# Four batches of sorted block attention and a token mixer on one core: another order of loads and work, V of one batch turned on TensorE, X of two batches turned by DMA

## The chip, the core and the metric

The kernel runs on one core of a Trainium2 chip. A core has five engines with queues of their own, each working strictly in order: PE (TensorE, matrix products), DVE (VectorE), ACT (ScalarE), POOL (GpSimd) and SP (SyncE, which here only issues transfers). [...] Loads that change the type are issued by POOL; all transfers run on 16 DMA engines. The metric is the device time of one execution in microseconds (us).

## The reference

There are B = 4 batches, H = 8 heads, S = 768 rows and D = 64. A row of 768 is cut into 8 blocks of 96.

```python
P = sort_net                                  # [4, 8, 8, 8]
for _ in range(5):
    P = P - max(P, -1); P = exp(P)
    P = P / (sum(P, -1) + 1e-09)
    P = P / (sum(P, -2) + 1e-09)
k_sorted = einsum('bhij,bhjcd->bhicd', P, k_blocks)      # the same for v
scores = (q_block @ k_sorted_block.T) / sqrt(D)          # 96 x 96 in each block
attn = softmax(scores)
x = (attn @ v_sorted_block)  -> [B, S, H*D]              # [4, 768, 512]

wq, wk = x @ w_q, x @ w_k                                # 64 columns each
mixed = (wq @ wk.T / sqrt(64)) @ x                       # 768 x 768, no softmax
out = relu(mixed) @ w_out                                # float32 [4, 768, 512]
```

The kernel computes `wq @ (wk.T @ x)`, with the 64 x 512 matrix in brackets first.

## The kernel before

The whole order of work is written out by hand in the string `ORDER`, and a loop at the end of the function calls one small function `u_<letter>` for each word. A word such as `K03:6` is a PE step: letter K, batch 0, index 3, first PSUM bank 6. A word such as `k03:A:6` is the step that empties that bank, on ACT (`A`) or DVE (`D`); `G` is POOL and `S` is SP. Since each engine works in order, `ORDER` is at once the queue of each engine: a step that waits holds all later steps of its own engine, and the others run on until they need it.

The steps of a batch, in the order in which data flows:

- `lq`, `lk`, `lv`: the load of Q, K or V of a batch (1.5 MB of float32 in memory, 768 KB as bf16) on POOL's queue into one of three buffers; `lp` loads w_q and w_k, `lo` w_out.
- `a`, `c`: the five rounds of normalizing P (exponential on ACT, the rest on DVE); `B` and `n` spread the result into the mask products M (128 x 128 for each head) which sort the blocks by a matrix product. `n00` to `n03` (batch 0) are on DVE, those of later batches on POOL.
- `Q`, `q`: Q turned on PE (12 products a step, for two heads) and copied to QT. `K`, `k`: K sorted and turned in one product with M, copied to KT. `S`, `e`: scores of five head-pair blocks, exponential on ACT into E.
- `V`, `v`: V sorted by M into Vs; `R`: six transfers a batch on SP's queue that regroup Vs into VT (rows of a block on the partitions). VT has a column of ones for the sums of the softmax. `N`: a copy of one column of VT on POOL, a gate that waits for the six transfers.
- `P`: E times VT, 14 products a step (8 in `P_4`); `r`, `x`: reciprocal of the sums and the scaled result into X on DVE.
- `T`, `t`: X turned on PE (8 products for a pair of heads) and copied to XT. `J`, `j`: wq and wk together into qkT; `d` copies the wq half to the other 64 partitions (qD). `W`, `w`, `G`, `g`: the 64 x 512 matrix. `H`, `h`: mixed and relu. `O`, `o`: product with w_out (4 products of 512 columns) and its copy to an output tile; `s`: the store.
- `i`: constants. `i00` makes the identity on POOL, `i02` some zeros on DVE, and `i03` on POOL the pads of E, the columns of ones in Vs and VT and a corner of Rall. `Z019` is 19 products of zeros that fill PE's queue.

Buffers of batch b are used again by batch b + 2, those of the loads (`Qn`, `Kn`, `Vn`) by batch b + 3. `u_Y`, `u_y`, `u_F`, `u_f` (L276 to L289) are in the file before the change, but no word of `ORDER` calls them. After the last step a guard on POOL (L438 to L449) checks the range of Rall and would run a slow general path; it does not here.

Of the kernel before, what the change touches and what calls it, by code (L numbers as in the profile page):

```python
# [9 lines left out]
BF16 = mybir.dt.bfloat16  # L10
# [4 lines left out]
NMIX = 2  # L15

ORDER = """
i02:D c00:D i00:G lq0 a01:A c01:D a02:A c02:D Z019:0 Q03:0 a03:A c03:D a04:A Q00:1 c04:D Q02:2 lq1
a05:A c05:D lv0 Z010:3 B00:3 lk0 n00:D:3 q00:A:1 n03:D:3 n02:D:3 Q13:1 i03:G Q11:4 q02:A:2 q03:D:0
Q12:2 q13:A:1 n01:D:3 Q01:5 Z011:6 V01:6 V00:0 q12:D:2 v00:A:0 u00:D:3 q01:D:5 V02:2 Q10:5 lk1  # L20
v02:A:2 Z09:0 K00:0 K01:2 n10:G q10:D:5 q11:A:4 K02:4 v01:A:6 K03:6 k00:A:0 lv1 k01:D:2 n11:G
k03:A:6 S00:0 k02:D:4 S01:2 S06:6 S04:4 e01:A:2 Z03:2 K10:2 e00:A:0 K13:0 e06:A:6 R01:S S02:6
k10:D:2 k13:D:0 K12:2 S05:0 e04:A:4 n21:G S03:4 R00:S R04:S e02:A:6 k12:D:2 lk2 e05:A:0 R03:S K11:6
lq2 e03:A:4 R02:S R05:S n20:G S14:2 e14:A:2 V12:0 k11:D:6 v12:D:0 V10:6 P03:4 r03:D:4 x03:D:4 V11:2
S11:0 v10:A:6 v11:A:2 P01:6 e11:A:0 P02:4 S12:2 S13:0 r01:D:6 x01:D:6 e12:A:2 r02:D:4 K22:6 k22:A:6
K20:2 e13:A:0 P04:6 x02:D:4 S15:4 e15:A:4 k20:D:2 P00:2 S10:0 r04:D:6 Q23:4 x04:D:6 R14:S r00:D:2
Q20:5 S16:6 e10:A:0 N05:G R15:S R10:S Q22:0 x00:D:2 Q21:3 q20:D:5 e16:A:6 K23:1 K21:5 T01:7 R11:S
q22:D:0 lv2 R12:S R13:S q23:A:4 k21:A:5 q21:D:3 lp k23:D:1 P12:3 t01:A:7 T02:0 r12:D:3 P11:5
x12:D:3 r11:D:5 V20:1 lq3 T03:7 t02:A:0 T00:0 V21:3 v20:A:1 x11:D:5 P13:1 t00:D:0 t03:A:7 P14:5
v21:A:3 r13:D:1 T11:7 J01:0 V22:3 x13:D:1 r14:D:5 j01:A:0 x14:D:5 P10:1 v22:A:3 r10:D:1 t11:D:7  # L30
n30:G x10:D:1 J00:0 S23:5 S20:3 T12:7 lk3 j00:A:0 e23:A:5 t12:D:7 e20:A:3 T13:0 W01:1 W00:2 n31:G
T10:5 S24:6 w01:D:1 t13:D:0 w00:D:2 S22:3 S25:0 t10:D:5 R23:S Q30:2 e24:A:6 Q31:5 Q33:6 N15:G G00:7
e22:A:3 q30:D:2 e25:A:0 Q32:2 d01:S K32:3 lv3 q31:D:5 q33:D:6 K31:5 K33:0 G01:7 q32:D:2 R20:S
k32:A:3 R24:S k31:A:5 k33:D:0 d00:S S21:2 J10:4 e21:A:2 g00:D:7 R25:S R21:S j10:D:4 S35:5 H02:0 lo
e35:A:5 R22:S H00:2 h00:A:2 J11:7 K30:4 j11:A:7 h02:D:0 k30:D:4 S32:0 W10:6 V30:2 w10:D:6 W11:7
V32:4 e32:A:0 P23:0 w11:A:7 v32:A:4 V31:6 v30:D:2 r23:D:0 v31:A:6 O04:2 x23:D:0 R31:S P20:3 S26:0
r20:D:3 R34:S S30:5 G10:7 G11:7 e26:A:0 S33:0 x20:D:3 H01:3 e30:A:5 o04:A:2 g10:D:7 P21:5 O05:2
h01:A:3 P22:3 d11:S r21:D:5 x21:D:5 T20:7 o05:A:2 e33:A:0 r22:D:3 t20:A:7 P24:5 R35:S x22:D:3
r24:D:5 O03:2 d10:S o03:A:2 O00:0 S36:3 H10:1 R32:S x24:D:5 S31:5 o00:A:0 R30:S e31:A:5 O02:7
h10:D:1 T22:0 e36:A:3 o02:A:7 t22:D:0 S34:5 s02:S H11:1 H12:3 R33:S T21:7 e34:A:5 N25:G O01:0  # L40
t21:A:7 P33:5 h11:D:1 T23:7 P30:1 h12:A:3 t23:A:7 o01:D:0 r33:D:5 P32:3 x33:D:5 s00:S r30:D:1 J20:0
O12:5 r32:D:3 s01:S P31:6 x30:D:1 j20:D:0 x32:D:3 O10:1 r31:D:6 O11:0 J21:4 j21:A:4 P34:2 x31:D:6
T32:6 o10:A:1 d21:S T31:7 r34:D:2 t31:A:7 T30:4 W20:1 N35:G x34:D:2 t30:A:4 T33:2 t32:D:6 t33:D:2
O15:3 J30:4 w20:D:1 W21:1 J31:2 j30:A:4 W30:4 j31:D:2 O14:7 W31:2 o11:A:0 w21:A:1 G20:1 o14:A:7
d30:D w30:A:4 s10:S d20:S G21:1 w31:D:2 G30:4 o15:A:3 G31:4 g20:A:1 o12:A:5 H20:6 h20:A:6 H22:2
H21:0 d31:D g30:D:4 h22:D:2 O13:4 O21:7 o13:A:4 s11:S h21:D:0 O20:6 o20:A:6 H30:2 s12:S H31:4
h31:A:4 o21:D:7 O24:7 O25:6 O22:4 h30:D:2 O23:5 O31:3 o25:A:6 o23:A:5 o24:D:7 s20:S o22:D:4 H32:0
O30:4 s22:S o31:D:3 O33:3 s21:S h32:D:0 o33:D:3 o30:A:4 O35:0 O34:1 o34:A:1 s31:S O32:3 s30:S
o35:D:0 o32:A:3 s33:S s35:S s34:S s32:S
"""  # L50


# [1 line left out]
def kernel(  # L54
# [91 lines left out]
    def mm(o, w, x, start=True, stop=True, t=False):  # L146
        nc.tensor.matmul(o, w, x, is_transpose=t, start=start, stop=stop, skip_group_check=True)  # L147

    def copy(e, o, i):
        if e == "A":  # L150
            nc.scalar.copy(o, i)  # L151
        else:
            nc.vector.tensor_copy(o, i)  # L153
# [7 lines left out]

    def u_a(b, n, e, bank):
        nc.scalar.activation(Pv, Pv, ACT.Exp)
        if n == 2:
            for j in range(NB):
                mm(PS[:, 7, 0:SP], idb, idb[:, j * SP:(j + 1) * SP], start=(j == 0), stop=(j == NB - 1))
            nc.scalar.copy(m_p, PS[:, 7, 0:SP])
        elif n == 3:
            nc.scalar.copy(Lx.rearrange("p a j s -> p (a j) s"),
                           idb[0:BH, 0:BH].unsqueeze(2).to_broadcast([BH, BH, SP]))  # L170

    def u_c(b, n, e, bank):
        if n == 0:
# [46 lines left out]
                                in_=src[b, h0:h1].rearrange("h (p r) d -> p h (r d)", p=P))  # L220

    def u_B(b, n, bank):

        for i in range(NB):
            g, x = divmod(i, BH // NB)
            mm(PS[:, bank, i * BH:(i + 1) * BH], Lx[:, x].rearrange("p j s -> p (j s)"),
               PbT[:, g * BH:(g + 1) * BH])
# [74 lines left out]
        ENG[e].dma_start(out=VT[b % 2].rearrange("(s r) i h x -> r s i (h x)", r=R6)[n],  # L302
                         in_=Vs[0][:, n].rearrange("p h e -> p (h e)"))

    def u_N(b, n, e, bank):

        nc.gpsimd.tensor_copy(gate[0:R6, :], VT[b % 2][0:R6, NB - 1, H - 1, 0:1])  # L307
# [111 lines left out]
    def oslot(b, n):  # L419
        return ot[(b * 3 + n // 2) % NOT]  # L420
# [4 lines left out]
    def u_s(b, n, e, bank):  # L425
# [220 lines left out]
```

## Time and profile before

| | |
|---|---|
| median of 3 runs | 111.21 us (110.87 to 113.28) |
| span of the profiled execution, first to last instruction | 109.3 us |
| mean granted PE clock over that span | 0.966 |
| first Q of batch 0 usable on PE | 8.97 us |
| K of batch 0 usable on PE | 21.1 us |
| first V step of batch 3 on PE | 62.88 us |
| last product on PE starts its group of 20 | 100.84 us |

The profile is that of one execution. Times are from its first instruction. Engines' busy times overlap. A row of the timeline reads: start, length, engine, line, operation, output and input, count, and in brackets how long the engine stood idle and what ended it. A row of a group reads: operation, shapes, count, then total busy time, mean length of one in ns, then idle time ahead of the group. Nearly every PE row has the line L147 and every copy L151 (ACT) or L153 (DVE), since these are helpers; the tiles' names tell the steps apart. The digits of the slices are tenths, 40 slices of 2.73 us.

The loads of before are issued by POOL in the order q0, q1, v0, k0, k1, v1, k2, q2, v2, w_q, w_k, q3, k3, v3, w_out, with `i03`, the products `n` and the gates between them.

### The profile page before, as it was taken

The numbers are of one execution on the slowest core, as the hardware profiler recorded it, in microseconds if no ns is written. First come the engines' busy times: TensorE is split into PE (matmuls) and PEld (weight loads), VectorE is DVE, ScalarE is ACT, GpSimd is POOL, SyncE is SP. The second block draws the span as 40 slices with busy tenths as digits, with TensorE's granted clock in tenths as the row PEclk, the third lists the DMA queues.
The fourth block names the chain that finished last, engine by engine and source line by source line (L and its number), as shares of the span: only waits on it lengthen the run. The fifth ranks groups of instructions, "written<-read, shape, count | busy, mean of one in ns | idle before, by whom it ended". The sixth has DMA issues, their size and how long they took to land.

```text
span 109.3 us, 3462 instructions
## 1 busy us (share of the span) xinstructions
PE 94.8 (87%) x1460; PEld 64.3 (59%) x1460; DVE 71.1 (65%) x140; ACT 67.6 (62%) x96; POOL 26.8 (24%) x46
## 2 busy tenths in 40 slices
PE   4997999986978759999959999999999993999950
PEld 2335557463767648897948687746858672443410
DVE  2676681060959984799956898778898431974720
ACT  4224314897589874698976998899706671463240
POOL 7960029069079700330000000000004700000000
PEclk9999999999599995999999999999999999999999
DMA  0899999999999999999999914670360050097872
GB/s 3 91 201 204 203 204 206 203 235 248 229 210 199 218 254 239 188 209 202 218 242 248 201 25 117 164 244 6 127 261 17 6 218 4 40 418 309 352 307 112
DMA packets 20225, 20.16 MB, mean 185 GB/s; under 512 B 2032, under 2 KB 18288, under 8 KB 20208
## 3 DMA queue, kind: packets, MB, share of 16 engines
q0 software_dynamic: 14064, 10.09, 61.1%
q1 hardware_dynamic: 6144, 9.84, 26.7%
q8 instruction: 11, 0.18, 0.6%
q14 instruction: 6, 0.05, 0.1%
HBM read 20.19 MB, written 6.29 MB: 242 GB/s over the span
## 4 chain that ended last, share of the span: by engine, by line
PE 53%; DMA 34%; POOL 5%; issue 2%; DVE 2%; ACT 1%; POOLq 0%; ACTq 0%; DVEq 0%
PE ps L147 53%; DMA Kn<-in_k_dram 15%; DMA Qn<-in_q_dram 14%; DMA qD<-qkT 4%; POOL Qn L219 2%; POOL M L240 1%; DVE QT L153 1%; DVE KT L153 1%; POOL Kn L219 1%; POOL Vn L219 1%; ACT ot L151 1%; POOL idb L191 0%; POOL idb L190 0%; POOLq L191 0%; DVE qkT L153 0%
## 5 line engine op out<-in xcount | busy, mean ns | idle before, releaser
L321 ACT ACTIVATE E<-ps 96x960 bf16<-96x960 f32 (+1 forms) x28 | 24.1, 898 | 5.2 <-PE ps L147 5.1
L147 PE MATMUL ps<-wo,mixT 128*128 128x512 bf16 x96 | 22.7, 379 | 0.0
L350 DVE TENSOR_TENSOR X<-ps,Rall 96x896 bf16<-96x896 f32 (+1 forms) x20 | 20.1, 1005 | 0.6
L151 ACT COPY ot<-ps 128x512 f32<-128x512 f32 x17 | 10.0, 588 | 8.7 <-PE ps L147 8.0
L147 PE MATMUL ps<-fil 128*128 128x512 bf16 x52 | 14.4, 433 | 0.4 <-ACT Vs L151 0.2
L153 DVE CAST KT<-ps 128x768 bf16<-128x768 f32 x10 | 9.4, 956 | 7.7 <-PE ps L147 7.5
L147 PEld LDWEIGHTS <-mixT 128*128 128x128 bf16 x96 | 8.6, 98 | 9.4 <-issue 0.6
L151 ACT CAST Vs<-ps 128x1024 bf16<-128x1024 f32 x10 | 9.9, 1019 | 4.2 <-PE ps L147 4.0
L147 PE MATMUL ps<-VT,E 96*128 96x65 bf16 x256 | 10.9, 193 | 1.0 <-DVE X L350 0.3
L147 PEld LDWEIGHTS <-E 96*128 96x128 bf16 x256 | 9.8, 97 | 2.8 <-issue 1.3
L147 PE MATMUL ps<-idb,Qn 128*64 128x128 bf16 x192 | 8.1, 244 | 3.3 <-DMA Qn<-in_q_dram 1.9
L240 POOL TENSOR_TENSOR M<-PTR,m_p 128x512 bf16<-128x512 bf16 x6 | 7.9, 1323 | 12.1 <-DVE PTR L153 8.4
L412 DVE TENSOR_SCALAR mixT<-ps 128x1024 bf16<-128x1024 f32 x7 | 8.5, 1222 | 3.0 <-PE ps L147 3.0
L147 PE MATMUL ps<-QT,KT 64*128 64x96 bf16 x256 | 10.0, 213 | 0.4 <-DVE KT L153 0.2
L153 DVE COPY QT<-ps 128x768 bf16<-128x768 bf16 x11 | 5.9, 553 | 6.7 <-PE ps L147 6.7
L307 POOL COPY gate<-VT 6x1 bf16<-6x1 bf16 x4 | 0.7, 177 | 38.3 <-DMA VT<-Vs 38.3
L147 PEld LDWEIGHTS <-fil 128*128 128x128 bf16 x52 | 5.4, 109 | 7.4 <-issue 3.4
L147 PEld LDWEIGHTS <-Qn 128*64 128x64 bf16 x192 | 6.7, 124 | 4.6 <-DMA Qn<-in_q_dram 2.7
L147 PE MATMUL ps<-M,Kn 128*64 128x128 bf16 x192 | 8.0, 238 | 1.6 <-DMA Kn<-in_k_dram 1.3
L147 PEld LDWEIGHTS <-KT 64*128 64x128 bf16 x256 | 6.9, 99 | 3.5 <-issue 1.9
L147 PEld LDWEIGHTS <-Kn 128*64 128x64 bf16 x192 | 6.7, 121 | 3.5 <-DMA Kn<-in_k_dram 2.2
L147 PE MATMUL ps<-idb,X 96*128 96x96 bf16 x128 | 7.5, 206 | 0.0
(74 smaller groups left out, 129.0 us busy)
## 6 DMA issues: line engine op xcount, KB each, us to landing
out_dram<-ot SPq DMA_DIRECT2D x9, 512.0 KB, 3.3
VT<-Vs SPq DMA_DIRECT2D x24, 132.0 KB, 6.4
Qn<-in_q_dram POOLq DMA_DIRECT2D x4, 768.0 KB, 12.8
Vn<-in_v_dram POOLq DMA_DIRECT2D x4, 768.0 KB, 14.9
Kn<-in_k_dram POOLq DMA_DIRECT2D x4, 768.0 KB, 18.1
out_dram<-ot SPq DMA_DIRECT2D x6, 256.0 KB, 2.0
wo<-in_moe_w_out_dram POOLq DMA_DIRECT2D x1, 512.0 KB, 17.4
qD<-qkT SPq DMA_DIRECT2D x6, 48.0 KB, 3.3
```

Source lines behind the costliest of these rows:

```text
L147: nc.tensor.matmul(o, w, x, is_transpose=t, start=start, stop=stop, skip_group_check=True)
L151: nc.scalar.copy(o, i)
L153: nc.vector.tensor_copy(o, i)
L219: nc.gpsimd.dma_start(out=t[b % NIN][:, h0:h1].rearrange("p h r d -> p h (r d)"), in_=src[b, h0:h1].rearrange("h (p r) d -> p h (r d)", p=P))
L240: ENG[e].tensor_tensor(out=M[b % 2][:, h0:h0 + hn], in0=src.unsqueeze(2).to_broadcast([P, hn, SP, NB]), in1=m_p.unsqueeze(1).unsqueeze(3). ...
L307: nc.gpsimd.tensor_copy(gate[0:R6, :], VT[b % 2][0:R6, NB - 1, H - 1, 0:1])
L321: nc.scalar.activation(E[b % 2][:, n, 0:2 * w * BLK].rearrange("p (t a c) -> p a t c", a=2, c=BLK), PS[0:BLK, bank:bank + 2, 0:w * BLK].re ...
L350: nc.vector.tensor_mul(xo.rearrange("p (a t d) -> p a t d", a=2, d=D), avps(bank, w)[:, :, :, 0:D], Rall[:, b, n, :, 0:w].unsqueeze(3).to_ ...
L412: nc.vector.tensor_relu(o, i)
```

## The change

1. POOL's queue: all of q0, k0, v0, q1, k1, v1, w_q, w_k, q2, k2, v2, w_out, q3 are issued first, then `i03`, then the products `n` of batch 1 and 2 with k3 and v3 between.
2. The gates `N` are gone; `P` waits for the transfers itself.
3. V of batch 0 takes the steps `Y`, `y`, `F`, `f`: sorted and turned by 48 products with M, copied to the KT buffer of the other batch, turned back by 32 products and copied to VT. The six transfers `R` of batch 0 and its `V`, `v` are gone.
4. X of batches 2 and 3 is turned by `D`, a transposing transfer from SP's queue for each pair of heads, in place of `T` and `t` (eight steps each).
5. `d` of batches 0 to 3 is a copy on DVE or POOL throughout; before, six of the eight were transfers on SP's queue.
6. The product and copy for `m_p` and the copy for `Lx` are words of `ORDER` (`B01`, `p00`, `p01`). The products of zeros go from 52 to 24.
7. The whole of `ORDER` is new, with other banks and another split of copies between ACT and DVE.

```diff
-i02:D c00:D i00:G lq0 a01:A c01:D a02:A c02:D Z019:0 Q03:0 a03:A c03:D a04:A Q00:1 c04:D Q02:2 lq1
-a05:A c05:D lv0 Z010:3 B00:3 lk0 n00:D:3 q00:A:1 n03:D:3 n02:D:3 Q13:1 i03:G Q11:4 q02:A:2 q03:D:0
...
+i00:G i02:D B01:0 lq0 Z08:1 c00:D lk0 p01:A a01:A p00:A:0 lv0 c01:D lq1 a02:A c02:D lk1 Z010:0 lv1 a03:A c03:D
+lp a04:A lq2 Q01:0 c04:D Q02:1 q01:A:0 Q03:2 lk2 Q00:3 q03:D:2 Z03:4 a05:A q00:A:3 lv2 c05:D Z03:0 lo q02:D:1
+lq3 B00:0 n03:D:0 i03:G n01:D:0 K03:1 n00:D:0 K01:3 n02:D:0 k03:A:1 u00:D:0 K00:5 k01:D:3 n11:G S05:0 k00:A:5
+S02:2 e05:A:0 n10:G S06:4 Y03:6 e02:A:2 S01:0 y03:D:6 e01:A:0 S00:2 Y01:6 e06:A:4 Y00:0 y01:D:6 e00:A:2 F03:4
+n20:G f03:A:4 F01:7 Q12:2 f01:D:7 y00:A:0 Q11:3 P04:4 q11:A:3 Q13:7 r04:D:4 Q10:6 x04:D:4 q12:A:2 F00:0
+q10:D:6 q13:A:7 Y02:3 f00:D:0 K02:5 y02:D:3 k02:A:5 lk3 P00:0 r00:D:0 S04:6 lv3 x00:D:0 P01:4 e04:A:6 S03:2
...
+D23:S e34:A:2 S35:0 G11:6 D22:S e35:A:0 S32:4 s02:S g10:D:6 S36:2 O03:7 e32:A:4 H11:0 o03:D:7 e36:A:2 P33:4
+h11:A:0 s01:S P31:6 r33:D:4 P32:2 x33:D:4 O12:0 r32:D:2 r31:D:6 H10:4 x32:D:2 o12:A:0 O13:1 h10:A:4 x31:D:6
+D32:S J20:0 P34:2 j20:D:0 J21:4 D31:S r34:D:2 d20:D P30:5 x34:D:2 j21:A:4 W20:0 O10:7 r30:D:5 d21:G D33:S
+w20:D:0 x30:D:5 W21:0 o10:A:7 G20:2 w21:D:0 D30:S o13:D:1 H12:3 G21:2 h12:D:3 s11:S O11:1 g20:A:2 H20:6
+o11:A:1 H21:4 h20:D:6 O15:3 h21:A:4 s10:S O14:2 o15:A:3 O21:7 o14:A:2 J31:6 s12:S o21:A:7 J30:5 j31:A:6 O22:7
...
-    gate = sb.tile([P, 1], BF16, name="gate")
...
         nc.scalar.activation(Pv, Pv, ACT.Exp)
-        if n == 2:
-            for j in range(NB):
-                mm(PS[:, 7, 0:SP], idb, idb[:, j * SP:(j + 1) * SP], start=(j == 0), stop=(j == NB - 1))
-            nc.scalar.copy(m_p, PS[:, 7, 0:SP])
-        elif n == 3:
-            nc.scalar.copy(Lx.rearrange("p a j s -> p (a j) s"),
-                           idb[0:BH, 0:BH].unsqueeze(2).to_broadcast([BH, BH, SP]))
+
+    def u_p(b, n, e, bank):
+        if n == 0:
+            copy(e, m_p, PS[:, bank, 0:SP])
+        else:
+            copy(e, Lx.rearrange("p a j s -> p (a j) s"),
+                 idb[0:BH, 0:BH].unsqueeze(2).to_broadcast([BH, BH, SP]))
...
     def u_B(b, n, bank):
-
+        if n == 1:
+            for j in range(NB):
+                mm(PS[:, bank, 0:SP], idb, idb[:, j * SP:(j + 1) * SP], start=(j == 0), stop=(j == NB - 1))
+            return
...
-    def u_N(b, n, e, bank):
-
-        nc.gpsimd.tensor_copy(gate[0:R6, :], VT[b % 2][0:R6, NB - 1, H - 1, 0:1])
-
...
+    def u_D(b, n, e, bank):
+        ENG[e].dma_start_transpose(out=XT[b % 2][:, n, :].rearrange("p (i c) -> p i c", i=NB),
+                                   in_=X[b % 2][:, n].rearrange("p i m -> p (i m)"))
+
...
-        if e == "S":
-            nc.sync.dma_start(out=o, in_=i)
+        if e == "G":
+            nc.gpsimd.tensor_copy(o, i)
```

More of the change, by code (lines that the diff above doesn't have):

```diff
@@ L17 @@
 ORDER = """
-i02:D c00:D i00:G lq0 a01:A c01:D a02:A c02:D Z019:0 Q03:0 a03:A c03:D a04:A Q00:1 c04:D Q02:2 lq1
-a05:A c05:D lv0 Z010:3 B00:3 lk0 n00:D:3 q00:A:1 n03:D:3 n02:D:3 Q13:1 i03:G Q11:4 q02:A:2 q03:D:0
[L20 to L47, printed above, removed]
@@ L48 @@
-O30:4 s22:S o31:D:3 O33:3 s21:S h32:D:0 o33:D:3 o30:A:4 O35:0 O34:1 o34:A:1 s31:S O32:3 s30:S
-o35:D:0 o32:A:3 s33:S s35:S s34:S s32:S
+i00:G i02:D B01:0 lq0 Z08:1 c00:D lk0 p01:A a01:A p00:A:0 lv0 c01:D lq1 a02:A c02:D lk1 Z010:0 lv1 a03:A c03:D
+lp a04:A lq2 Q01:0 c04:D Q02:1 q01:A:0 Q03:2 lk2 Q00:3 q03:D:2 Z03:4 a05:A q00:A:3 lv2 c05:D Z03:0 lo q02:D:1
+lq3 B00:0 n03:D:0 i03:G n01:D:0 K03:1 n00:D:0 K01:3 n02:D:0 k03:A:1 u00:D:0 K00:5 k01:D:3 n11:G S05:0 k00:A:5
+S02:2 e05:A:0 n10:G S06:4 Y03:6 e02:A:2 S01:0 y03:D:6 e01:A:0 S00:2 Y01:6 e06:A:4 Y00:0 y01:D:6 e00:A:2 F03:4
@@ new lines @@
+n20:G f03:A:4 F01:7 Q12:2 f01:D:7 y00:A:0 Q11:3 P04:4 q11:A:3 Q13:7 r04:D:4 Q10:6 x04:D:4 q12:A:2 F00:0
+q10:D:6 q13:A:7 Y02:3 f00:D:0 K02:5 y02:D:3 k02:A:5 lk3 P00:0 r00:D:0 S04:6 lv3 x00:D:0 P01:4 e04:A:6 S03:2
+n21:G r01:D:4 e03:A:2 K10:0 x01:D:4 F02:7 k10:A:0 f02:D:7 K12:2 S10:0 k12:A:2 P03:6 V12:4 e10:A:0 r03:D:6
+V10:2 x03:D:6 v10:A:2 P02:0 v12:D:4 T03:7 T00:6 R10:S t03:A:7 V11:2 r02:D:0 t00:D:6 R14:S K13:4 v11:A:2
+x02:D:0 R15:S K11:6 n31:G k13:A:4 R11:S k11:D:6 T02:0 R12:S n30:G S16:1 S14:3 t02:A:0 R13:S S12:5 T01:7
@@ new lines @@
+e12:A:5 Q20:0 t01:D:7 q20:A:0 J00:7 e14:A:3 S13:5 j00:D:7 J01:0 e13:A:5 d00:D S15:3 j01:D:0 W00:7 e15:A:3
+Q21:6 d01:G w00:D:7 W01:0 q21:D:6 e16:A:1 Q23:7 w01:A:0 K23:3 q23:A:7 K22:1 K20:5 k22:D:1 k23:A:3 G00:7
+k20:D:5 Q22:0 S26:1 q22:A:0 P13:3 S20:5 e26:A:1 r13:D:3 G01:7 x13:D:3 e20:A:5 S24:0 g00:A:7 S25:5 e24:A:0
+P12:3 e25:A:5 r12:D:3 V20:0 x12:D:3 v20:A:0 V22:6 P14:4 v22:A:6 H00:2 R20:S r14:D:4 K21:0 x14:D:4 R21:S
+h00:A:2 V21:6 R24:S H01:4 v21:D:6 k21:A:0 R25:S O01:3 h01:A:4 S22:0 R22:S o01:D:3 S23:6 e22:A:0 T13:2 R23:S
@@ new lines @@
+S21:4 T12:3 e23:A:6 S11:0 t12:D:3 e11:A:0 Q32:6 Q31:3 q32:D:6 Q30:7 t13:A:2 q31:D:3 P10:0 q30:A:7 Q33:6
+r10:D:0 P11:2 x10:D:0 q33:A:6 O00:7 e21:A:4 r11:D:2 x11:D:2 H02:0 O02:6 o00:A:7 h02:D:0 s00:S T10:7 o02:A:6
+T11:2 P24:3 t10:A:7 t11:D:2 P22:5 r24:D:3 P21:0 x24:D:3 J11:7 r22:D:5 r21:D:0 x22:D:5 K31:2 j11:A:7 O05:4
+k31:A:2 d11:D x21:D:0 W11:5 K33:6 w11:A:5 K30:2 o05:D:4 k33:A:6 D21:S P20:0 J10:5 k30:A:2 r20:D:0 x20:D:0
+V32:6 j10:A:5 V30:2 v32:A:6 d10:D V31:4 D20:S v30:D:2 K32:0 v31:A:4 R35:S S31:6 k32:D:0 R34:S S30:2 e31:A:6
@@ new lines @@
+P23:4 R33:S S33:0 e30:A:2 r23:D:4 R32:S W10:6 x23:D:4 O04:7 R30:S e33:A:0 w10:D:6 R31:S S34:2 o04:A:7 G10:6
+D23:S e34:A:2 S35:0 G11:6 D22:S e35:A:0 S32:4 s02:S g10:D:6 S36:2 O03:7 e32:A:4 H11:0 o03:D:7 e36:A:2 P33:4
+h11:A:0 s01:S P31:6 r33:D:4 P32:2 x33:D:4 O12:0 r32:D:2 r31:D:6 H10:4 x32:D:2 o12:A:0 O13:1 h10:A:4 x31:D:6
+D32:S J20:0 P34:2 j20:D:0 J21:4 D31:S r34:D:2 d20:D P30:5 x34:D:2 j21:A:4 W20:0 O10:7 r30:D:5 d21:G D33:S
+w20:D:0 x30:D:5 W21:0 o10:A:7 G20:2 w21:D:0 D30:S o13:D:1 H12:3 G21:2 h12:D:3 s11:S O11:1 g20:A:2 H20:6
@@ L50 @@
+o11:A:1 H21:4 h20:D:6 O15:3 h21:A:4 s10:S O14:2 o15:A:3 O21:7 o14:A:2 J31:6 s12:S o21:A:7 J30:5 j31:A:6 O22:7
+d31:D j30:A:5 d30:D W31:6 W30:5 o22:D:7 O20:4 w31:A:6 w30:D:5 G30:5 o20:D:4 H22:6 G31:5 s20:S h22:A:6 O23:4
+g30:A:5 O24:7 o23:D:4 H30:5 s21:S o24:D:7 H31:3 h30:A:5 O25:2 h31:D:3 H32:0 o25:A:2 O30:7 h32:D:0 s22:S O32:6
+o30:A:7 O34:0 s30:S o32:A:6 O33:7 s32:S o34:D:0 O31:6 s34:S o33:D:7 O35:0 s33:S o31:A:6 s31:S o35:A:0 s35:S
 """
@@ L609 @@
         b, n = int(name[1]), int(name[2:])
-        if kind.isupper() and kind not in "RN":
+        if kind.isupper() and kind not in "RD":
             fns[kind](b, n, int(arg[0]))
```

## The prediction

> **What bounds the kernel now.** I read the page's busy line and slices first, then the chain of waits in order of time, then busy time by stretch.
>
> ```profile
> PE 94.8 (87%) x1460; PEld 64.3 (59%) x1460; DVE 71.1 (65%) x140; ACT 67.6 (62%) x96; POOL 26.8 (24%) x46
> PEclk9999999999599995999999999999999999999999
> DMA  0899999999999999999999914670360050097872
> ```
>
> PE is busiest, but its share is an average. The DMA digit is 9 from the third slice to the 23rd, so up to about 60 us the loads stream without a gap; from there PE is full. The clock digit falls to 5 twice, at 27 and 41 us, both times beside a wait for a load (below).
>
> ```profile
> 4.36 16.73 DMA Kn<-in_k_dram
> 24.93 15.54 DMA Qn<-in_q_dram
> 63.68 23.30 PE ps L147 x353
> 87.55 4.50 DMA qD<-qkT
> 92.09 13.25 PE ps L147 x75
> ```
>
> The chain waits for K of batch 0 until 21.09 us, then for Q of batch 2 until 40.47, then runs on PE with one break for the qD transfer. Three stretches of before, cut at K10 (26.4), V30 (62.88) and P33 (76.60), and the end behind the last matmul:
>
> ```profile
> 26.40:62.88 36.48, 31.96 (x707) 26.78 (x707) 28.19 (x46) 28.09 (x35) 9.81 (x13) 0.91 1.29 220
> 62.88:76.60 13.72, 13.70 (x224) 9.48 (x222) 11.33 (x17) 12.51 (x19) 0.18 (x1) 1.00 0.38 110
> 76.60:105.33 28.73, 26.99 (x265) 15.66 (x263) 18.55 (x30) 13.11 (x23) 3.23 (x7) 1.00 0.45 180
> 105.33:109.30 3.97, 0.00 (x0) 0.00 (x0) 0.00 (x0) 0.59 (x1) 0.00 (x0) 0.93 0.51 194
> ```
>
> Columns: length, then PE, PEld, DVE, ACT, POOL busy, clock, DMA, GB/s. In the second stretch PE is never idle and ACT is busy 12.51 of 13.72 us, 91%: two engines are nearly full there, and ACT has little to give.
>
> **The change, stage by stage.** I split the new kernel at P04 (the first P on PE) and at P33.
>
> *Start to P04.* Rows for the loads and POOL's queue:
>
> ```profile
> 1.48 2.03 POOL L219 DMA_DIRECT2D Qn<-in_q_dram  x2 [0.17 <-issue]
> 8.97 1.03 PEld L147 LDWEIGHTS <-Qn 128*64 128x64 bf16 x36 [1.27 <-DMA Qn<-in_q_dram]
> 12.82 1.37 PEld L147 LDWEIGHTS <-Qn 128*64 128x64 bf16 x48 [0.19 <-DMA Qn<-in_q_dram]
> 5.22 0.32 POOL L200 MEMSET E<- 96x224 bf16 x1
> 6.27 0.90 POOL L219 DMA_DIRECT2D Kn<-in_k_dram  x1
> 12.77 1.09 DVE L240 TENSOR_TENSOR M<-ps,m_p 128x256 bf16<-128x256 f32 x3 [0.85 <-PE ps L147]
> ```
>
> q0 is usable at 8.97 and q1, next in the queue, at 12.82: 3.85 us a load; up to k0, the fourth, it is (21.09 - 8.97)/3 = 4.04. With q0, k0, v0 ahead, k0 lands at about 12.9 instead of 21.1, just as the mask products M (12.77) are ready. So the long first wait goes, and E of batch 0 is done some 7 us sooner. What is late next is on POOL. The memsets i03, issued at 5.22 before, now stand behind lq3. In the built program the loads share eight completion counters in turn, so lq3, the thirteenth, waits for the fifth, k1: 8.97 + 4 x 3.85 to 4.04 = 24.4 to 25.1. Its issue takes 0.90 and the memsets 6.27 - 5.22 = 1.05, so they end at 26.4 to 27.1; I take 26.5. P04 reads the columns of ones in VT and waits for them. All else on PE stands behind P04: Q13, Q10, F00, Y02, K02, and so S04 and the next E. V of batch 0 by Y and F (48 + 32 matmuls for 24) and the 28 fillers taken out lie in this idle time and cost nothing; the six R transfers of batch 0 go as well. If P04 did not wait, Y and F would still be hidden, because q1 lands only at 8.97 + 3 x 3.85 = 20.5.
>
> M of batch 1 stands behind lq3 too, and the gates are gone:
>
> ```profile
> 15.60 1.31 POOL L240 TENSOR_TENSOR M<-PTR,m_p 128x512 bf16<-128x512 bf16 x1 [8.43 <-DVE PTR L153]
> L307 POOL COPY gate<-VT 6x1 bf16<-6x1 bf16 x4 | 0.7, 177 | 38.3 <-DMA VT<-Vs 38.3
> VT<-Vs SPq DMA_DIRECT2D x24, 132.0 KB, 6.4
> ```
>
> n11 and n10 end at 26.5 + 2 x 1.31 = 29.1; K10, the first to use them, stands behind S03 and can't start before 30.7, so they are hidden. The gates made POOL wait 38.3 us off the path and held lv2 and later loads behind the R transfers; now P waits for the six transfers itself and the loads run beside them. R of batch 1 is issued from about 37 and takes 6.4 us and some more, P13 comes near 47: hidden.
>
> The price of the fillers is the clock: the two low slices follow idle times of 1.05 and 1.13 us in these rows, and here PE stands for about 5 us.
>
> ```profile
> 26.42 1.14 PE L147 MATMUL ps<-M,Kn 128*64 128x128 bf16 x24 [1.05 <-DMA Kn<-in_k_dram]
> 40.51 1.49 PE L147 MATMUL ps<-idb,Qn 128*64 128x128 bf16 x24 [1.13 <-DMA Qn<-in_q_dram]
> 57.69 1.19 PE L147 MATMUL ps<-M,Kn 128*64 128x128 bf16 x36
> ```
>
> 24 matmuls take 1.14 us in the low slice, 36 take 1.19 at full clock. From P04 to S04 PE has 88 (8+12+12+8+12+12+14+10): 2.9 us at the one pace, 4.2 at the other. I take the slow one: ACT gets its next E at 26.5 + 4.2 = 30.7. [...]
>
> *P04 to P33.* At 26.5 the two kernels have PE work of about the same size behind them (fillers apart), but not the same ACT work ahead. From 26.5 to P33 the new order gives ACT 20 long and 3 short E, 9 KT, 6 QT, 6 Vs, 4 XT, 3 ot, 2 mixT, 2 qkT and three small copies.
>
> ```profile
> L321 ACT ACTIVATE E<-ps 96x960 bf16<-96x960 f32 x24 | 22.6, 967 | 2.8 <-PE ps L147 2.7
> L321 ACT ACTIVATE E<-ps 96x384 bf16<-96x384 f32 x4 | 1.9, 484 | 2.4 <-PE ps L147 2.4
> L151 ACT CAST KT<-ps 128x768 bf16<-128x768 f32 x6 | 4.7, 800 | 3.2 <-PE ps L147 3.2
> L151 ACT COPY QT<-ps 128x768 bf16<-128x768 bf16 x5 | 3.9, 791 | 1.8 <-PE ps L147 1.8
> L151 ACT CAST Vs<-ps 128x1024 bf16<-128x1024 f32 x10 | 9.9, 1019 | 4.2 <-PE ps L147 4.0
> L151 ACT COPY XT<-ps 128x768 bf16<-128x768 bf16 x8 | 6.3, 806 | 0.1
> L151 ACT COPY ot<-ps 128x512 f32<-128x512 f32 x17 | 10.0, 588 | 8.7 <-PE ps L147 8.0 <-ACT wk L151 0.8
> L410 ACT ACTIVATE mixT<-ps 128x1024 bf16<-128x1024 f32 x5 | 5.1, 1028 | 2.3 <-PE ps L147 2.3
> L151 ACT CAST qkT<-ps 128x384 bf16<-128x384 f32 x5 | 2.4, 478 | 5.7 <-PE ps L147 5.6
> ```
>
> At busy time over count: 18.8 + 1.4 + 7.1 + 4.7 + 5.9 + 3.2 + 1.8 + 2.0 + 1.0, and 1.1 for the small ones (three, bounded by 0.5 each) = 47.0 us, against 28.09 + 12.51 = 40.6 in before's stretch from K10 to P33. PE's share there was 31.96 + 13.70 = 45.7 with nearly the same items, so ACT is the fuller of two full engines, and DVE has less. E36 (0.5) is not needed for P33 and q13 and k02 (1.6) run before 30.7; 44.9 us are left. At 91%, the rate of before's fullest stretch, they take 49.4; with no gaps 44.9; I take 94%, 47.8, since ACT is now the engine in front rather than the one behind. P33 then starts at 30.7 + 47.8 = 78.5 (75.6 to 80.1), against 76.60 before. The loads do not bound it: the same bytes, less six R transfers, end near 60 as before, and Q20, K23, V20 and Q32 come after their loads by several us at ACT's pace.
>
> *P33 to the end.* Of PE's items behind P33 the new order lacks five T and has two H more; all else is the same, 18 O among it.
>
> ```profile
> L147 PE MATMUL ps<-idb,X 96*128 96x96 bf16 x128 | 7.5, 206 | 0.0
> L147 PE MATMUL ps<-qkT,Ab 64*128 64x256 bf16 x24 | 3.9, 271 | 0.0
> 92.09 0.28 PE L147 MATMUL ps<-qD,Ab 64*128 64x256 bf16 x1 [1.74 <-DMA qD<-qkT]
> ```
>
> T: 40 x 7.5/128 = -2.3; H: 4 pairs x 3.9/24 = +0.65; the qD wait of 1.74 goes, since d20 and d21 are now copies on DVE and POOL. 28.73 - 2.3 + 0.65 - 1.74 = 25.3 us, then the same 3.97. What could come late instead are the transposing transfers: J20 needs D22 and D23, J31 needs all four of batch 3. D30 waits for x30. P30's place puts that some 7.5 us behind P33 (three pairs r, x on DVE, then r34, x34, then r30, x30), at 86.2, and J31 stands about 11.7 us of PE work behind P33, at 90.2.
>
> ```profile
> out_dram<-ot SPq DMA_DIRECT2D x6, 256.0 KB, 2.0
> qD<-qkT SPq DMA_DIRECT2D x6, 48.0 KB, 3.3
> ```
>
> No trace shows a transposing transfer. By bytes, 192 KB, the nearest rows are 2.0 us for 256 KB and 3.3 for the 48 KB between partitions; by pieces it writes 128 x 8 lines, as many as a load has packets, at 3.85 us apiece. I take 3.3 from issue to landing, and that four in a row follow each other faster than that: D30 lands at 89.5, just hidden. D22 and D23 are issued early, behind R31, and have more room. [...]
>
> Sum: 78.5 + 25.3 + 4.0 = 107.8 us of span, 1.5 below 109.3. The median of the runs, 111.21, lies 1.9 above the profiled span; so 109.7.
>
> **Rivals.** *ACT does not bind, or POOL does not hold P04.* With no gaps on ACT P33 comes at 75.6, the span is 104.9, the time 106.8. If lq3 were issued without waiting, P04 would follow Q11 at about 21.5; M for batch 1, two products on POOL, would then be early too, and the end could move by up to 5 us, to 104.7. For it: ACT does 91% where it isn't even first. Against: banks are reused at once, so a late copy on either engine stops PE, and the wait on the fifth counter stands in the program.
>
> *The transposes are slow, and the kernel is slower.* At 3.85 us each, one behind the other on SP's queue, with D32 issued when x31 is done (about 83), four take to 98.4 and J31 starts 8 us late: time 118. It decides from about 1.75 us apiece. [...] Against: SP's queue holds little else then, and the loads are over.
>
> *The order costs more than it moves.* ACT at before's 77% (28.09 of 36.48) would put P33 at 89 and the time at 120; that stretch waited for loads, so little speaks for it.
>
> **How the numbers follow.** A 2% step (what a measurement here can tell from no change) is a time of 109.0 or 113.4. Chances: the forecast 0.45, most of it inside 2%, a third of it faster; first rival 0.22; slow transposes 0.25, with some of it inside 2%; poor ACT 0.08. So faster 0.37, same 0.33, slower 0.30. Eight in ten: from 105.0 (first rival with some of both parts) to 116.5 (transposes at some 3.5 us). The forecast's own range is 107 to 112.
>
> **What would show it.** P04 waits for POOL until 26 to 27; then ACT with hardly a gap to 78; no PE wait for DMA from 30 us on; J20 and J31 without a wait for the transposes. Wrong if PE waits there, or if a load is late for Q32 or V32.

## The result and the profile after

The changed kernel is slower.

| | before | after |
|---|---|---|
| median of 4 runs, us | 112.25 (110.87 to 113.36) | 114.25 (113.9 to 114.35) |
| ratio to before, 95% interval | 1 | 1.028 (1.024 to 1.033) |
| span of the profiled execution, us | 109.3 | 112.5 |
| first P33 on PE, us | 76.60 | 81.56 |
| from P33 to the last product on PE, us | 28.73 | 26.49 |
| from there to the end, us | 3.97 | 4.45 |

The ratios leave out executions over 1.5% longer than the fastest of their kernel: here two of the four of before (113.28 and 113.36 us), and among the experiments also the profiled ones of e11 and e13.

So the 3.2 us of span are 5.0 lost ahead of P33, 2.2 won back behind it and 0.5 lost after the last product. The time lost is to be sought ahead of P33. The page's busy line and clock digits of the changed kernel:

```profile
PE 90.8 (81%) x1415; PEld 60.5 (54%) x1424; DVE 67.9 (60%) x136; ACT 71.0 (63%) x101; POOL 26.8 (24%) x44
PEclk9999999975559999999999999999999999999999
```

PE has 4.0 us less to do than before and yet the end is later. The clock is low in one place only, a slice at 0.7 and three at 0.5 in a row, of 2.81 us each; cut finely, it is 0.50 from 23.80 to 34.03 us. Before, there were two single slices. POOL's timeline of the changed kernel (start, length, engine, line, operation, output and input, idle time before it and what ended that) shows what happens there:

```profile
9.31 0.89 POOL L214 DMA_DIRECT2D Qn<-in_q_dram  x1 [0.84 <-DMA Qn<-in_q_dram]
13.15 0.88 POOL L214 DMA_DIRECT2D Kn<-in_k_dram  x1 [2.95 <-DMA Kn<-in_k_dram]
16.98 0.88 POOL L214 DMA_DIRECT2D Vn<-in_v_dram  x1 [2.96 <-DMA Vn<-in_v_dram]
21.35 0.75 POOL L209 DMA_DIRECT2D wo<-in_moe_w_out_dram  x1 [3.50 <-DMA Qn<-in_q_dram]
26.04 0.89 POOL L214 DMA_DIRECT2D Qn<-in_q_dram  x1 [3.93 <-DMA Kn<-in_k_dram]
26.91 0.30 POOL L195 MEMSET E<- 96x224 bf16 x1
...
27.60 0.38 POOL L201 MEMSET VT<- 96x128 bf16 x2
```

The ninth load is issued when the first has landed, the tenth when the second has, and so on: the thirteenth, lq3, stands until k1, the fifth, is there. The `i03` memsets come behind it and end at about 27.9. The idle time in brackets is of no matter to POOL, which has nothing else to do; it matters to PE, whose timeline at the three places where it stands longest after 21 us reads:

```profile
27.89 0.60 PE L142 MATMUL ps<-VT,E 96*128 96x65 bf16 x8 [5.91 <-POOL VT L201]
...
51.23 0.59 PE L142 MATMUL ps<-VT,E 96*128 96x65 bf16 x14 [1.27 <-DMA VT<-Vs]
...
81.56 1.46 PE L142 MATMUL ps<-VT,E 96*128 96x65 bf16 x42 [1.05 <-DMA VT<-Vs]
```

These are P04, P13 and P33. P04 waits 5.91 us for a memset that depends on nothing. The chain of waits of the changed kernel tells the same in order of time:

```profile
5.20 20.30 DMA Kn<-in_k_dram
...
27.89 5.35 PE ps L142 x78
...
42.92 8.17 DMA VT<-Vs
...
78.83 2.59 DMA VT<-Vs
```

Before, the chain's first wait was for K of batch 0 until 21.09; now it is for K of batch 1 until 25.50, and the way from there to PE is POOL's queue, not the data. The stretches that the prediction cut, with their columns (length, busy PE, PEld, DVE, ACT and POOL, clock, DMA, GB/s), from P04 to the next E on ACT, to P33, to the last product, to the end:

```profile
27.89:33.87 5.98, 5.97 (x91) 5.08 (x91) 3.67 (x7) 1.60 (x3) 5.13 (x7) 0.50 1.40 200
33.87:81.56 47.69, 42.60 (x856) 32.00 (x861) 33.78 (x54) 43.13 (x57) 4.99 (x5) 1.00 0.83 163
81.56:108.05 26.49, 26.29 (x229) 13.59 (x232) 16.83 (x28) 12.31 (x22) 3.74 (x8) 1.00 0.72 230
108.05:112.50 4.45, 0.00 (x0) 0.00 (x0) 0.00 (x0) 0.58 (x1) 0.00 (x0) 1.00 0.42 163
```

The first stretch runs wholly at half the clock. In the second PE is busy 89% and ACT 90% of the time. The transposing transfers (all eight on SP: shortest, median and longest time in SP's queue in ns; below, from issue to landing) are quick:

```profile
L356 SPq DMA_TRANSPOSE XT<-X x8: 1212/1240/1332, 71.0 to 89.0; - x8
...
DMA to landing us min/median/max: 2.6/2.7/4.1
```

### The profile page after: what moved, and what is told of

Same layout as the page of the kernel before. It is cut to its first block, busy times and chain, and to the rows that moved or that the text cites. A ratio compares the mean times of both kernels' runs of the same rounds, so it can differ in the third digit from the quotient of the medians.

```text
span 112.5 us, 3357 instructions
## 1 busy us (share of the span) xinstructions
PE 90.8 (81%) x1415; PEld 60.5 (54%) x1424; DVE 67.9 (60%) x136; ACT 71.0 (63%) x101; POOL 26.8 (24%) x44
## 4 chain that ended last, share of the span: by engine, by line
PE 39%; DMA 28%; ACT 10%; DVE 6%; issue 6%; POOL 5%; SPq 3%; POOLq 0%; DVEq 0%; ACTq 0%
PE ps L142 39%; DMA Kn<-in_k_dram 18%; DMA VT<-Vs 10%; ACT E L314 7%; SPq L300 3%; DVE X L343 2%; POOL Qn L214 2%; DVE Vs L148 1%; DVE Rall L338 1%; ACT Vs L146 1%; ACT mixT L407 1%; POOL Kn L214 1%; POOL Vn L214 1%; ACT KT L146 1%; DVE VT L148 1%
## 5 line engine op out<-in xcount | busy, mean ns | idle before, releaser
L146 ACT COPY ot<-ps 128x512 f32<-128x512 f32 x14 | 8.2, 588 | 8.4 <-PE ps L142 8.3
L146 ACT COPY QT<-ps 128x768 bf16<-128x768 bf16 x10 | 7.9, 804 | 8.0 <-PE ps L142 7.9
L338 DVE RECIPROCAL Rall<-ps 96x14 f32<-96x14 f32 (+1 forms) x20 | 4.3, 224 | 13.6 <-PE ps L142 12.9
L146 ACT CAST KT<-ps 128x768 bf16<-128x768 f32 x12 | 9.3, 801 | 4.9 <-PE ps L142 4.8
L142 PEld LDWEIGHTS <-KT 64*128 64x128 bf16 (+1 forms) x288 | 8.7, 100 | 5.5 <-issue 2.5
L370 POOL COPY qD<-qkT 64x384 bf16<-64x384 bf16 x2 | 1.0, 500 | 43.3 <-ACT qkT L146 40.1
L148 DVE COPY ot<-ps 128x512 f32<-128x512 f32 x10 | 6.9, 689 | 5.1 <-PE ps L142 5.0
L148 DVE CAST KT<-ps 128x768 bf16<-128x768 f32 x8 | 7.5, 952 | 3.5 <-PE ps L142 3.4
L407 ACT ACTIVATE mixT<-ps 128x1024 bf16<-128x1024 f32 x7 | 7.3, 1044 | 3.1 <-PE ps L142 3.1
L142 PE MATMUL ps<-fil 128*128 128x512 bf16 x23 | 7.8, 510 | 0.2 <-issue 0.2
```

Of the source, the lines that this page charges most:

```text
L338: nc.vector.reciprocal(Rall[:, b, n, :, 0:w], avps(bank, w)[:, :, :, D])
L370: nc.gpsimd.tensor_copy(o, i)
L407: nc.scalar.activation(o, i, ACT.Relu)
```

## The experiments

Each ratio is to the kernel before, run on the same chip in the same session, with its 95% interval.

### POOL's hold, in two parts

e1 moves the memsets alone, to a place ahead of the first load that waits:

```diff
 lp a04:A
+i03:G
 lq2
...
 lq3 B00:0 n03:D:0
-i03:G
 n01:D:0
```

> The changed kernel with one word moved: the memsets i03 stand ahead of the load of Q of batch 2 on POOL's queue, not behind that of Q of batch 3. Theory (the hold of P04 is a loss on the path): P04 starts at about 22 instead of 27.89, the next E at 28 to 30 instead of 33.87 (M of batch 1 still stands behind the load of Q of batch 3 and ends near 29.5, which K10 may wait for), and most of it arrives at the end: 110 to 112 us against 114.3. Rival (the hold is absorbed, since a load, a transfer or ACT sets P33 anyway): P04 moves and P33 stays within 1 us of 81.56, 113.5 to 114.5 us.

Measured: 0.994 (0.987 to 1.001), span 109.3. PE's timeline of e1, at P04, K10 and P33:

```profile
21.92 0.42 PE L142 MATMUL ps<-VT,E 96*128 96x65 bf16 x8
...
29.28 0.85 PE L142 MATMUL ps<-M,Kn 128*64 128x128 bf16 x12 [2.64 <-POOL M L238]
...
78.32 1.46 PE L142 MATMUL ps<-VT,E 96*128 96x65 bf16 x42 [0.71 <-DMA VT<-Vs]
```

P04 no longer waits at all and comes 6.0 us sooner. But the span shrinks by only 3.2, since a second step stood behind the same load: M of batch 1 on POOL, for which K10 now waits 2.64 us. In the changed kernel that wait lay hidden behind the first. The clock goes down at this wait too (0.50 from 27.67 to 34.50).

e2 also takes the loads out of the way of M:

```diff
 lp a04:A
+i03:G
 lq2
...
-lo
 q02:D:1
-lq3
 B00:0 n03:D:0
-i03:G
 n01:D:0
...
 e05:A:0 n10:G
+lo lq3
 S06:4
```

> As the kernel with the memsets first, and the two products M of batch 1 and then w_out and Q of batch 3 follow in that order, so that M of batch 1 waits for no load but V of batch 0: it ends near 20.5 instead of 30.6. Theory: P04 at 22, the next E at 27 to 28, P33 5 us earlier, 108.5 to 110.5 us. Rival (M of batch 1 is not on the path): the same as with the memsets alone, within 0.5 us. Rival (nothing of POOL's hold matters): 113.5 to 114.5 us.

Measured: 0.970 (0.964 to 0.975), span 106.6. POOL's timeline of e2: the memset of VT, then M of batch 1 ahead of the load that used to hold it:

```profile
9.09 0.44 POOL L201 MEMSET VT<- 96x128 bf16 x2
...
18.00 2.57 POOL L238 TENSOR_TENSOR M<-PTR,m_p 128x512 bf16<-128x512 bf16 x2
...
25.49 0.88 POOL L214 DMA_DIRECT2D Qn<-in_q_dram  x1 [3.27 <-PE ps L142]
```

lq3 is issued at 25.49 instead of 26.04, so the load itself loses nothing by standing later in the queue. Three words of the order in other places, with nothing else changed, are worth 5.9 us of span and turn a loss of 2.8% into a gain of 3.0%. The stretch from the next E to P33 of e2 shows why it is not the full 7.5 us by which that E comes earlier (26.40 against 33.87):

```profile
26.40:75.62 49.22, 43.96 (x855) 33.13 (x859) 33.98 (x54) 42.82 (x57) 7.53 (x7) 0.97 1.03 188
```

PE is busy 1.36 us longer for the same products, at a clock of 0.97 instead of 1.00; the stretch is 1.53 longer. Behind P33 the two kernels take the same, 31.0 and 30.9 us.

### The clock after the hold

e5 keeps the hold and fills it with 26 products of zeros:

```diff
 Q11:3
+Z026:4
 P04:4
```

> The changed kernel with 26 products of zeros put on PE ahead of P04, about 5.6 us at full clock, in the time in which PE stood still. Theory (the stretch from P04 to the next E, 5.98 us at a granted clock of 0.50, is long because PE had stood still): clock near 1.0 there, the stretch 4 to 4.5 us, 112.5 to 113.2 us. Rival (its length is set by copies and waits): 5.5 us or more, 114 to 114.6 us.

Measured: 1.014 (1.008 to 1.019), span 111.6. The windows from P04 to the next E, and PE's timeline at P13, of e5:

```profile
28.11:32.01 3.90, 3.60 (x93) 3.10 (x92) 3.31 (x7) 1.60 (x3) 3.90 (x4) 1.00 1.41 201
```

```profile
49.99 0.59 PE L142 MATMUL ps<-VT,E 96*128 96x65 bf16 x14 [1.99 <-DMA VT<-Vs]
```

The same products take 3.90 us in place of 5.98: the low clock cost 2.1 us of the restart. Of these, 0.9 reach the span (111.6 against 112.5), one reason being that P13 then waits 1.99 us for its transfers instead of 1.27. In e2, where nothing is idle there, that stretch is also 3.90 us long. In the changed kernel PE has the clock of 0.50 for 6.14 us behind P04, until 34.03.

### Does ACT set the stretch to P33?

e3 gives five of ACT's copies to DVE, e10 leaves them on ACT and does each twice:

```diff
-q20:A:0 ... q23:A:7 ... q22:A:0 ... v20:A:0 ... q30:A:7
+q20:D:0 ... q23:D:7 ... q22:D:0 ... v20:D:0 ... q30:D:7
```

```diff
-q20:A:0 ... q23:A:7 ... q22:A:0 ... v20:A:0 ... q30:A:7
+q20:A:0 q20:A:0 ... q23:A:7 q23:A:7 ... q22:A:0 q22:A:0 ... v20:A:0 v20:A:0 ... q30:A:7 q30:A:7
```

> The changed kernel with five copies (q20, q23, q22, v20, q30) on DVE instead of ACT: ACT has 4.2 us less between the first E behind P04 and P33, DVE 3.4 us more. Theory (ACT sets the length of that stretch, busy 43.1 of 47.7 us): P33 comes 2.5 to 4 us earlier, 110.5 to 112 us. Rival (the stretch is set by the banks and the order of PE, ACT's load is a sign and no cause): P33 within 0.7 us, 113.6 to 115 us.

> The changed kernel with the same five copies (q20, q23, q22, v20, q30) done twice on ACT, 4.2 us more of ACT between the first E behind P04 and P33. Theory formed after the run with these copies on DVE (PE's own work and its waits for R set the stretch, ACT follows with some room): P33 0.5 to 2 us later, 114.5 to 116 us. Rival (the forecast's: ACT sets it): P33 about 4 us later, 117.5 to 118.5 us.

Measured: e3 1.023 (1.014 to 1.032), span 111.9; e10 1.035 (1.027 to 1.043), span 114.7. The windows from the next E to P33, of e3 and then of e10:

```profile
33.67:80.96 47.29, 42.43 (x855) 32.00 (x860) 36.84 (x59) 39.45 (x52) 5.14 (x5) 1.00 0.85 166
```

```profile
33.84:83.72 49.88, 43.23 (x856) 32.45 (x861) 33.86 (x54) 46.65 (x62) 4.97 (x5) 1.00 0.80 156
```

With 3.7 us less on ACT (43.13 to 39.45) the stretch is 0.4 shorter; were ACT the bound, it would be about 3.7 to 4 shorter. With 3.5 more it is 2.2 longer. So ACT is not what sets the stretch as a whole, but stands close enough behind to set it when it grows. The step is not quite clean, since DVE has 3.1 us more to do in e3 (33.78 to 36.84), and ACT is not off the path either: in the changed kernel's chain of waits 6.6 of the 9.0 us from 52.19 to 61.22 are pieces on ACT. e11 makes e3's edit on e2:

> The kernel with POOL freed, and the five copies on DVE instead of ACT. Theory (PE sets the time): within 0.6 us of 108.2. Rival (with POOL's hold gone ACT is the limit): 1.5 to 3 us faster, 105 to 106.7 us.

Measured: 0.974 (0.961 to 0.987), no better than e2's 0.970. With POOL out of the way, taking work off ACT gains nothing either.

### The transposing transfers against PE

e9 is e2 with `T` and `t` back in the places of the eight `D`:

```diff
-D21:S
+T21:0 t21:D:0
...
-D30:S
+T30:5 t30:D:5
```

> The kernel with POOL freed (memsets first, M of batch 1 ahead of the load of Q of batch 3), but X of batches 2 and 3 turned by T on PE and copied by t, at the places and in the order of the D words. Theory (D takes 3.75 us off PE, which is full behind P33): 2.5 to 4.5 us slower than with D, 110.7 to 112.7 us. Rival (the time is set by waits between engines, and PE has room): within 1 us of 108.2.

Measured: 1.021 (1.010 to 1.032), span 111.8 against e2's 106.6; P33 at 77.96 against 75.62. Eight more turns on PE and their copies cost 5.2 us, more than expected. Some of that is the place: PE waits there four times for a copy `t` and once for the x ahead of a T, 0.48 to 0.89 us each and 3.3 us in all, waits that e2 does not have.

e4 puts `D` into the order of before, in the places of `T` for batches 2 and 3, without the copies `t`:

```diff
-T20:7 ... t20:A:7 ... T22:0 ... t22:D:0 ... T33:2 ... t33:D:2
+D20:S ... D22:S ... D33:S
```

> The kernel before with one part of the change alone: X of batches 2 and 3 turned by the transposing transfer D, each word D at the place of the T that it replaces, no t copies. Theory (T and t cost PE up to 64 x 7.5/128 = 3.75 us where it is full, D is hidden where it has room): 1 to 3 us faster than before, with a wait at J30, which follows the last turn of X closely here and D lands 2.7 us after its issue. Rival (D lands too late for J20 and J30 in this order): no change or up to 2 us slower.

Measured: 1.048 (1.031 to 1.066), span 115.0. SP's and PE's timelines of e4:

```profile
70.33 1.59 SPq L359 DMA_TRANSPOSE XT<-X  x1
71.98 0.57 SPq L298 DMA_DIRECT2D VT<-Vs  x1
72.60 0.59 SPq L373 DMA_DIRECT2D qD<-qkT  x1
```

```profile
74.73 0.39 PE L143 MATMUL ps<-qD,Ab 64*128 64x256 bf16 x1 [1.97 <-DMA qD<-qkT]
...
91.05 0.65 PE L143 MATMUL ps<-XT,wqk 128*128 128x384 bf16 x3 [2.92 <-DMA XT<-X]
```

Here SP's queue carries `D`, R and qD together: a `D` takes 1.2 to 1.6 us of it, with R and qD behind, and J of batch 3 waits 2.92 us for XT. At each of these two waits the clock goes to 0.50 as well (74.68 to 78.09 and 91.75 to 95.16). The transfer itself is no slower than in the changed kernel: its median from issue to landing is 2.7 us in both. So the same transfer that is worth about 5% in one order costs 5% in another; the waits point to what else is in its queue and to how far its reader stands behind it, which no run varies one at a time.

### The copies of qD, and the gates

e6 does the six qD transfers of before as copies, as the change does; e7 drops the gates `N` of before.

```diff
-d01:S ... d00:S ... d11:S ... d10:S ... d21:S ... d20:S
+d01:G ... d00:D ... d11:D ... d10:D ... d21:G ... d20:D
```

```diff
-N05:G ... N15:G ... N25:G ... N35:G
```

> The kernel before with one part of the change alone: the six qD transfers are copies on DVE (four) and POOL (two). Theory (the only cost of the transfers on the path is the wait of PE of 1.74 us at 92.09): 1.2 to 1.8 us faster. Rival (PE then waits for the next thing, the copy of Ab or mixT): within 0.6 us.

> The kernel before without the four gates on POOL; P waits for the six transfers itself and the loads are no longer held behind R. Theory (the gates hold back loads only where there is room): within 0.7 us. Rival (the gates keep loads out of the way of R, and R lands later without them): P of batch 0 waits for DMA, 1 to 3 us slower. A third: loads come earlier without the gates, 1 to 3 us faster.

Measured: e6 0.970 (0.958 to 0.982), span 106.2, with P33 at 75.64; e7 0.997 (0.987 to 1.006). The gates are worth nothing that can be told, though a P of batch 1 then waits 1.73 us for R (at 45.14). The kernel with the copies is 3.1 us of span faster than before, more than the wait of 1.74 that went: P33 comes 1.0 sooner as well. Whether the copies did that too is not shown: one thing that PE no longer has ahead of P33 is a stop of 1.28 us at 56.11 in which it waited for nothing that the profile shows, and e7, whose qD go as transfers too, has only 0.50 of it. This one part of the change, on the kernel before, gives as much as the whole new order with POOL freed (e2, also 0.970).

e12 asks the reverse, on e2: the six copies as transfers again.

```diff
-d00:D ... d01:G ... d11:D ... d10:D ... d20:D ... d21:G
+d00:S ... d01:S ... d11:S ... d10:S ... d20:S ... d21:S
```

> The kernel with POOL freed, with the six qD copies as transfers on SP's queue again, as in the kernel before. Theory (those transfers stall PE in any order, and share SP with D here): 1.5 to 4 us slower, 109.7 to 112.2 us. Rival (the steps H stand far enough behind in this order): within 0.8 us of 108.2.

Measured: 0.952 (0.942 to 0.962), span 104.8: the fastest of all, where my theory expected a loss against e2. Part of the difference from e2 is the clock. The windows from P13, behind its wait for R (1.25 and 1.23 us), to P24, of e2 and then of e12:

```profile
43.70:61.17 17.47, 15.53 (x281) 11.62 (x284) 11.30 (x17) 14.81 (x19) 0.00 (x0) 0.90 1.24 229
```

```profile
43.35:59.76 16.41, 14.46 (x280) 10.39 (x283) 11.30 (x17) 14.71 (x19) 0.00 (x0) 1.00 1.27 223
```

The same products keep PE busy 1.07 us longer in e2, at 0.90, and that is all of the 1.06 us by which its stretch is longer. Nothing shows that the transfers kept the clock up in e12. Another 0.96 us is gained behind P33 (30.02 against 30.98), but not on PE: from P33 to the last product both take 26.5. It lies behind the issue of the last store (2.6 us to the end against 3.5), and its cause is open.

### V of batch 0

e13 is e2 with V of batch 0 by `V`, `v` and six `R` instead of `Y`, `y`, `F`, `f`:

```diff
-Y03:6 ... y03:D:6 ... Y01:6 ... Y00:0 y01:D:6 ... F03:4 ... f03:A:4 F01:7 ...
+V00:6 ... v00:D:6 R00:S R01:S ... V01:6 ... V02:0 v01:D:6 R02:S R03:S ... v02:A:0 R04:S R05:S
```

> The kernel with POOL freed, with V of batch 0 by V, v and the six transfers R as in the kernel before, in place of Y, y, F, f. Theory (turning V of batch 0 on PE is what lets P04 start at 22.5: the six transfers beside the loads take 6 us and more): P04 at 27 to 29, 3 to 6 us slower than with Y and F, 111 to 114 us. Rival (the start of batch 0 is not on the path, later waits swallow it): within 1 us of 108.2.

Measured: 1.051 (1.027 to 1.075). PE's timeline of e13 at P04:

```profile
31.05 0.60 PE L142 MATMUL ps<-VT,E 96*128 96x65 bf16 x8 [7.78 <-DMA VT<-Vs]
```

The regrouping transfers run beside the loads, and PE waits 7.78 us for them. Behind that wait the clock stays at 0.50 for 12.0 us more, to 43.09. With V turned on PE there is no such wait (e2: 0.970).

The load order alone, without the rest of the new order, was not tried, so its own worth is open.

## Why the prediction was wrong

Its sum against the trace, in us of span:

| step | forecast | measured | error |
|---|---|---|---|
| start to P04 | 26.5 | 27.89 | +1.4 |
| P04 to the next E on ACT | 4.2 | 5.98 | +1.8 |
| next E to P33 | 47.8 | 47.69 | -0.1 |
| P33 to the last product | 25.3 | 26.49 | +1.2 |
| the end | 3.97 | 4.45 | +0.5 |
| span | 107.8 | 112.5 | +4.7 |

**Start to P04, the step that failed most together with the restart.** The mechanism was forecast and e1 and e2 show it: lq3 waits for k1, `i03` stands behind lq3, P04 behind `i03`. The size was short: "they end at 26.4 to 27.1; I take 26.5". I stepped from q0 by 3.85 to 4.04 us a load and came to 24.4 to 25.1 for the fifth; it landed at 25.50, and lq3 was issued only at 26.04, 0.54 us later, a step that the sum did not have. A row quoted in the prediction itself would have told this without any stepping: K10 of before at 26.42, which waited for the same k1, then too the fifth load of the queue; with the 0.90 and 1.05 of the sum it gives 28.4, 0.5 over instead of 1.4 under. A time read off the same event beats a rate run on over four loads.

**The restart.** "2.9 us at the one pace, 4.2 at the other. I take the slow one" for 88 products. Two things were short. At full clock this stretch takes 3.90 us (e2, e5) and not 2.9, as it isn't made of the kind of product that I took the pace from; and the low clock lasted over all of the 5.98 us, 2.1 more than at full clock, where I had put 1.3. The slow pace was also misread: the row at 26.42 is not one at the low clock, for over 26.42 to 27.49 the granted clock was 0.70 on average. The row quoted below it, 40.51, was at 0.50 throughout; its 24 products take 1.43 us until the next row starts, which for 88 makes 5.2. How long the clock stays low behind a wait was my estimate alone: it was at 0.50 for 6.14 us behind P04 here and for 12.0 us behind the wait of e13. What brings it back is not shown.

**P04 to P33.** The length was right within 0.1 us by luck, and its reason was wrong. "ACT is the fuller of two full engines" does not stand as the bound of the stretch after e3 and e10. ACT had 43.1 us to do, not 44.9, at 90% and not 94%: two errors that cancel. What sets the stretch instead is bounded, not settled: PE is busy 42.60 of the 47.69 us, waits 1.27 for R at P13 and 1.05 at P33, where the prediction had R as hidden and named a PE wait for DMA from 30 us on as a sign of being wrong, and ACT stands close behind. This matters for the sign of the advice: from the forecast one would have unloaded ACT, which gives 0.6 us; unloading POOL's queue gives 5.9.

**P33 to the end.** Half of the 1.2 us is the term T, -2.3 us for 40 products at their mean busy time. The busy times of these products overlap, those of the first row here with the next row's by 0.16 us. What counts is their spacing, on PE's timeline of before:

```profile
82.83 1.18 PE L147 MATMUL ps<-idb,X 96*128 96x96 bf16 x24
83.85 0.39 PE L147 MATMUL ps<-idb,qkT 128*96 128x128 bf16 x4
```

24 of them take 1.02 us until the next group starts, so 40 take 1.7, not 2.3. The wait for qD went, as forecast. The other half is spread over products that the sum took as unchanged: from start to start, the 32 of G (wk and X) take 2.24 us instead of 1.87 and the 64 of P 2.21 instead of 2.00, and PE stands idle for 0.20. Why they are spaced wider here is open. The 0.5 at the very end lies behind the issue of the last store (3.5 us to the end, 2.9 before), where no engine computes. It is no property of this order alone, for e12 with the same last steps takes 2.6; its cause is open.

**What was hidden.** The transposes were forecast at 3.3 us and hidden, and landed in 2.6 to 4.1 with a median of 2.7; no product waited for XT from them. The gates and the fillers' other places cost nothing, as forecast, with the one exception of the hold, where 26 fillers would have bought 0.9 us of span (e5). V of batch 0 by `Y` and `F` was hidden, and e13 shows that it is worth more than hidden.

**The rivals.** The second half of the first one, P04 without POOL's hold at "about 21.5" and up to 5 us gained, is what e2 makes: P04 at 22.50 and 5.9 us. (Its time is 108.2 us and not the rival's 104.7, which was counted from a forecast that was itself short.) As the kernel stands it did not happen, since the hold is real; it is what the change gives once the hold is taken out of it. The slow transposes did not come true in either order: in e4 they land as fast, and what costs there is SP's queue and a reader close behind.

**The sign.** The forecast stood 1.5 us of span below before, with errors of one sign in four of five terms; 3.2 us in the hold and its restart alone were enough to turn it. Why is the change, which removes a wait of some 8 us at the start and eight T from PE, not faster? The wait was not removed but moved, from K of batch 0 at 21.1 us to a memset at 27.9 behind K of batch 1, with the clock gone low in it.

## What to carry to other kernels

A queue that issues loads can be held by an earlier load's completion (lq3 here for 3.93 us by k1); work that other engines need, however small, belongs ahead of the first load that waits, and one that hides behind another shows only when the first is moved (e1, then e2). When a change moves the order of everything, date each event from a row of the same event before stepping there by a rate, price a pipelined product by its spacing, and take a pace from a row that lies wholly in one state of the clock. Replacing an engine's work by a transfer paid in one order here and cost in the other (e9, e4), so it has to be judged in the order where it will stand. And a change of many parts is worth taking apart: one part alone on the kernel before (e6) gained what the whole did not.

## What the hardware did that I had not expected

- In the changed kernel the clock fell to 0.50 at 23.80, 1.8 us into an idle time of 5.91 us, and stayed there over 6.14 us of nearly gapless products; 26 fillers ahead of P04 kept it at 1.00.
- Four low stretches, at 0.50, are of 3.41 or 3.42 us: 26.84 to 30.26 and 40.50 to 43.91 before, 18.10 to 21.52 and 45.41 to 48.82 in e2. The one of e1, 27.67 to 34.50, is of 6.83 us, twice as long, and that of the changed kernel, 23.80 to 34.03, of 10.23, three times. Why is not shown.
- Behind a wait of 1.25 us in e2 the mean clock was 0.90 over 17.47 us; behind one of 1.23 us at the same place in e12 it was 1.00 over 16.41 us. The length of the wait alone doesn't tell the two apart; I leave it open.
- The transfers R took 8.17 us on the chain at 42.92, while loads ran, and 2.59 us at 78.83, when they were over.
- A transposing transfer held SP's queue for 1.24 us in the changed kernel (median), about twice as long as the 0.57 to 0.59 us of the R and qD transfers shown of e4.
